# Attention and top-1 experts on one core: score columns packed, and the order of TensorE written over pairs of heads

## The chip, the core and the metric

One NeuronCore of one Trainium2 chip runs the whole program. The metric is the device time of one execution in microseconds. Three runs of the kernel before gave 333.72, 333.74 and 530.59 us; the median is 333.74 us.

## The reference

Four batches of eight heads attend over 768 tokens with 64 values a head; then every token passes a gate to one of eight experts. `is_retrieval` is `[1, 0, 1, 0, 0, 0, 1, 0]`: heads 0, 2 and 6 see all earlier keys ("full" heads here), the other five see the last 64 keys and the first four, the sinks ("streaming" heads).

```python
scores = scale * np.matmul(q, k.transpose(0, 1, 3, 2))
causal = rel >= 0
stream_keep = causal & (is_sink | in_win)     # is_sink: key < 4, in_win: rel < 64
...
a = np.exp(scores)
a = a / (np.sum(a, axis=-1, keepdims=True) + 1e-09)
out = np.matmul(a, v)
...
x = out.transpose(0, 2, 1, 3).reshape(B * S, H * D)
do_compute = (x @ w_skip) > 0
e_idx = np.argmax(x @ w_gate, axis=1)         # of the tokens in do_compute
h = np.maximum(xc[mask] @ w1[e], 0.0)
y[mask] = gate_w[mask, None] * (h @ w2[e])
out[do_compute] = xc + y
```

## The kernel before

The function `tile_duo_attention_split__then__moe_early_exit_skip_kernel` works in three stages.

**Attention** (lines 369 to 513) loops over four batches and, in each, over four pairs of heads, sixteen pairs in all. GpSimd issues the loads of q and k with a cast to fp16 (lines 378 and 381) and, for every second pair, two tiles of expert weights of 1 MB each, cast likewise (lines 415 and 416), all on its one DMA queue. SyncE (SP) issues the loads of v in fp32 (line 384) and the stores of a batch's output (line 516). TensorE (PE) transposes q and k, 24 small transposes a pair (line 392); ScalarE (ACT) copies qT (line 399), VectorE (DVE) kT (line 403), GpSimd casts v (line 409).

For each head, `qk_exp` takes one key block of 128 and a stretch of up to 512 queries: a matmul gives the scores in PSUM with the keys along the partitions (line 433, tile `pst`, two buffers), ScalarE takes the exponential into `ats` (line 439), VectorE multiplies the blocks on the diagonal and beside it with masks (lines 442 and 465). A streaming head has for each key block its own and the next query block, and a row group of its own for the four sink keys, 4 rows by 512 queries. Then line 484 weighs: for each query block the matmuls of `ats` with v and a column of ones add up in `opsa`, and VectorE divides (lines 491 and 492).

After each pair GpSimd casts the output (line 498), PE transposes it (line 503), and line 510 adds the pair's part to the gate's logits. After each batch VectorE chooses experts and gives every token a place in a list of 256 slots per expert (lines 518 to 589).

**Routing** (lines 591 to 623) turns the lists into gather and scatter indices (`idx_g` in line 611, `idx_s` in line 613).

**Experts** (lines 625 to 690): GpSimd gathers sixteen tiles of 128 tokens (line 636); `first(e)` casts and transposes tokens (line 652) and multiplies with `w1` (line 662); `second(e)` multiplies with `w2` (line 673), adds to the tokens on VectorE (line 677), and scatters the rows back (line 679). Each scatter waits for the one before. `general_path` is taken only if a list overflows or `is_retrieval` differs; with these inputs it is not.

The order of the work on each engine is set by a scheduler that follows the order of the code and what is ready; pools with a number of buffers limit how far it runs ahead.

## Time and profile before

| what | value |
|---|---|
| median of 3 runs | 333.74 us |
| profiled execution, its own time | 336.85 us |
| its span, first to last instruction | 335.3 us |
| PE busy | 260.9 us, 78% |
| DVE busy | 150.0 us, 45% |
| ACT busy | 123.9 us, 37% |
| POOL busy | 102.7 us, 31% |
| read from HBM, written | 56.64 MB, 10.49 MB |

The span is from the first to the last instruction on the core; the time of an execution also holds what lies around it. A busy share is a mean over stages that differ, so the stages are read one by one. The ends of matmuls are modelled; their starts are measured.

### The profile page before, as it was taken

What the parts mean: (1) busy time and instruction counts of PE and PEld (TensorE: products, weight loads), DVE (VectorE), ACT (ScalarE), POOL (GpSimd) and SP (SyncE); (2) the same over time, 40 slices, a digit from 0 to 9 for tenths busy, and PEclk for the clock granted to TensorE, in tenths of its full rate; (3) what the DMA queues carried; (4) which work ended last, traced back from release to release, by engine and by line L of the source; (5) the groups of instructions that cost most, each with busy time, mean ns of one, the idle gap of its engine ahead of it and who ended that gap; (6) DMA issues with size and microseconds to landing.
All of it is one profiled execution on the core that took longest, in us unless ns stands there. A gap on an engine that the chain in (4) does not pass through costs nothing.

```text
span 335.3 us, 5082 instructions
## 1 busy us (share of the span) xinstructions
PE 260.9 (78%) x1844; PEld 144.6 (43%) x1844; DVE 150.0 (45%) x619; ACT 123.9 (37%) x289; POOL 102.7 (31%) x161
## 2 busy tenths in 40 slices
PE   0297999966999995899998599995318899999600
PEld 0143645532445543354454244443215667776200
DVE  1223553438554554747435855644821244332300
ACT  1054454424654551645353455552002232333000
POOL 8920241443224326032131020200067523222320
PEclk9999999999999999999999999999999999999955
DMA  6999979799999999999743600002346601110010
GB/s 95 145 204 204 198 126 189 123 217 229 207 204 195 202 197 228 259 203 195 122 87 57 203 1 0 3 0 80 111 128 188 186 18 73 48 71 32 18 38 2
DMA packets 53122, 42.64 MB, mean 127 GB/s; under 512 B 27931, under 2 KB 44315, under 8 KB 53090
## 3 DMA queue, kind: packets, MB, share of 16 engines
q0 software_dynamic: 24864, 29.66, 48.1%
q1 hardware_dynamic: 28226, 12.59, 16.6%
q8 instruction: 16, 0.26, 0.3%
q14 instruction: 16, 0.13, 0.1%
HBM read 56.64 MB, written 10.49 MB: 200 GB/s over the span
## 4 chain that ended last, share of the span: by engine, by line
PE 60%; DMA 15%; DVE 7%; ACT 5%; POOL 5%; issue 5%; POOLq 0%; DVEq 0%; ACTq 0%
PE pst L433 18%; PE opsa L484 14%; DMA qin<-in_q_dram 8%; PE hps L662 7%; DMA out_dram<-xg,idx_s 6%; PE yps L673 5%; ACT ats L439 5%; PE kTps L392 5%; PE qTps L392 4%; PE gxtp L503 3%; PE gps L510 1%; DMA xg<-out_dram,idx_g 1%; PE xtp L652 1%; POOL va L409 1%; POOL gx L498 1%
## 5 line engine op out<-in xcount | busy, mean ns | idle before, releaser
L439 ACT ACTIVATE ats<-pst 128x256 f16<-128x256 f32 (+4 forms) x236 | 91.5, 418 | 95.3 <-PE pst L433 93.6
L433 PE MATMUL pst<-qT,kT 64*128 64x256 f16 (+4 forms) x236 | 88.8, 426 | 6.1 <-ACT ats L439 3.9
L484 PE MATMUL opsa<-va,ats 128*128 128x65 f16 x552 | 66.6, 240 | 3.7 <-ACT ats L439 2.5
L484 PEld LDWEIGHTS <-ats 128*128 128x128 f16 x552 | 38.7, 116 | 59.9 <-DVE ats L442 16.8
L409 POOL CAST va<-vf 128x768 f16<-128x768 f32 x16 | 13.7, 859 | 87.8 <-PE opsa L484 40.5
L665 ACT ACTIVATE ht<-hps 128x512 f16<-128x512 f32 x32 | 18.9, 598 | 55.7 <-PE hps L662 51.5
L392 PE MATMUL qTps<-ident,qin 128*64 128x128 f16 x192 | 22.7, 314 | 16.1 <-DMA qin<-in_q_dram 16.1
L662 PE MATMUL hps<-xT,w1a 128*128 128x256 f16 x256 | 31.7, 286 | 1.9 <-issue 1.9
L673 PE MATMUL yps<-w2a,ht 128*128 128x512 f16 x128 | 29.9, 379 | 0.5 <-DVE xg L677 0.5
L442 DVE TENSOR_TENSOR ats<-ats,retr_diag 128x128 f16<-128x128 f16 x72 | 16.1, 239 | 31.7 <-ACT ats L439 31.4
L433 PEld LDWEIGHTS <-kT 64*128 64x128 f16 (+1 forms) x236 | 19.3, 102 | 25.0 <-issue 15.2
L662 PEld LDWEIGHTS <-w1a 128*128 128x128 f16 x256 | 26.3, 103 | 7.6 <-issue 2.1
L679 POOL DMA_INDIRECT out_dram<-xg,idx_s x16 | 15.9, 995 | 43.3 <-DMA out_dram<-xg,idx_s 30.1
L392 PE MATMUL kTps<-ident,kin 128*64 128x128 f16 x192 | 26.8, 314 | 3.0 <-DMA kin<-in_k_dram 3.0
L442 DVE TENSOR_TENSOR ats<-ats,strm_dn 128x128 f16<-128x128 f16 x100 | 24.9, 249 | 7.6 <-ACT ats L439 6.9
L677 DVE SCALAR_TENSOR_TENSOR xg<-yps,gsl,xg 128x512 f32<-128x512 f32 x16 | 11.9, 750 | 36.3 <-PE yps L673 36.3
L498 POOL CAST gx<-xb 128x768 f16<-128x768 f32 x16 | 13.3, 831 | 47.8 <-DVE xb L492 47.8
L392 PEld LDWEIGHTS <-qin 128*64 128x64 f16 x192 | 15.6, 161 | 20.1 <-DMA qin<-in_q_dram 16.7
L392 PEld LDWEIGHTS <-kin 128*64 128x64 f16 x192 | 17.0, 159 | 11.0 <-issue 6.0
L636 POOL DMA_INDIRECT xg<-out_dram,idx_g x16 | 16.6, 1036 | 15.8 <-DVE idx_s L613 11.2
L403 DVE COPY kT<-kTps 128x768 f16<-128x768 f16 x16 | 15.3, 958 | 12.4 <-PE kTps L392 10.3
L491 DVE RECIPROCAL rec<-opsa 128x6 f32<-128x6 f32 x32 | 6.3, 196 | 28.0 <-PE opsa L484 27.3
(123 smaller groups left out, 227.2 us busy)
## 6 DMA issues: line engine op xcount, KB each, us to landing
w1a<-in_moe_w_dram POOLq DMA_DIRECT2D x8, 1024.0 KB
w2a<-in_moe_w_dram POOLq DMA_DIRECT2D x8, 1024.0 KB
vf<-in_v_dram SPq DMA_DIRECT2D x32, 192.0 KB, 9.0
out_dram<-xb SPq DMA_DIRECT2D x4, 1536.0 KB, 7.6
qin<-in_q_dram POOLq DMA_DIRECT2D x16, 192.0 KB
kin<-in_k_dram POOLq DMA_DIRECT2D x16, 192.0 KB
xg<-out_dram,idx_g POOLq DMA_INDIRECT x16
out_dram<-xg,idx_s POOLq DMA_INDIRECT x16
```

The costliest lines, as they stand in the source:

```text
L392: nc.tensor.matmul(dn[hd * D:(hd + 1) * D, n], src[:, hd, n * D:(n + 1) * D], C.ident, is_transpose=True, start=(n == 0), stop=(n == NQB - 1))
L409: nc.gpsimd.tensor_copy(va[:, :, :, :D], vf)
L433: nc.tensor.matmul(pst[:k_rows, :qn], kTh[:, j * P:j * P + k_rows], qTh[:, q_lo:q_hi], start=True, stop=True)
L439: nc.scalar.activation(dst, pst[:k_rows, :qn], ACT.Exp)
L442: nc.vector.tensor_mul(ats[:k_rows, sl, q_lo:q_lo + mw], ats[:k_rows, sl, q_lo:q_lo + mw], diag_mask[:k_rows, :mw])
L484: nc.tensor.matmul(opsa[:, i, :], ats[:kr, sl, i * QB:i * QB + QB], vh[:kr, j, :], start=(cnt == 1), stop=(cnt == total))
L498: nc.gpsimd.tensor_copy(x16, xb[:, :, h0:h0 + 2].rearrange("p n h d -> p n (h d)"))
L636: nc.gpsimd.indirect_dma_start(out=xg, out_offset=None, in_=out[:, :], in_offset=bass.IndirectOffsetOnAxis(ap=idx_g[:, t:t + 1], axis=0), ...
L662: nc.tensor.matmul(hps[:, fi, :], w1a[:, e, s, fs * P:(fs + 1) * P], xT[:, s, :], start=(s == 0), stop=(s == DS - 1))
L665: nc.scalar.activation(ht[:, 2 * f2:2 * f2 + 2], hps, ACT.Relu)
L673: nc.tensor.matmul(yps, hts[e][:, fs, s2 * P:(s2 + 1) * P], w2a[:, e, fs, :], start=(fs == 0), stop=(fs == FS - 1))
L679: nc.gpsimd.indirect_dma_start(out=out[:, :], out_offset=bass.IndirectOffsetOnAxis(ap=idx_s[:, t:t + 1], axis=0), in_=xgs[t], in_offset=No ...
```

## The change

Scores are packed. A full head's 21 blocks of 128 by 128 lie one after another in 2688 columns, the six diagonal blocks first; a streaming head's eleven blocks in 1408. They are computed in chunks of 1024 columns, each with one exponential, and the tile `pst` holds 1024 columns, two buffers as before. For a streaming head the four sink keys take over the first four rows of the blocks beside the diagonal (keys there that the window leaves out), and `vx` is v with its first four rows changed to match; so there is no row group for the sinks, and their weighting matmuls are gone. One mask instruction covers a chunk of a streaming head, or the six diagonal blocks of a full one.

q and k are loaded in fp32 by SP, two pairs of buffers, and cast by GpSimd with both heads side by side, so that one transpose of 128 by 128 serves both heads: 12 a pair. The transposes of q and k, of the gate and the counts of the routing share one PSUM buffer (`tps`).

The order on PE is written out over pairs: in iteration i stand the scores of pair i, the transposes of pair i + 1, the weighting of pair i - 1 and the gate of pair i - 2. The other engines are ordered by the scheduler. Output is stored by half batches. The weight tiles are tiles of their own; `load_weights` asks for them as the loop goes, and the last expert's two tiles lie in a pool that opens after attention. Two of five masks move into `general_path`, the rest are built after the first casts.

```diff
-    C.retr_diag = band_mask(nc, const, "retr_diag", 0, 0, None)
-    C.strm_d0 = band_mask(nc, const, "strm_d0", 0, 0, WINDOW - 1, sink=True)
-    C.strm_dn = band_mask(nc, const, "strm_dn", 0, 0, WINDOW - 1)
-    C.strm_s0 = band_mask(nc, const, "strm_s0", QB, 0, WINDOW - 1, sink=True)
-    C.strm_sn = band_mask(nc, const, "strm_sn", QB, 0, WINDOW - 1)
-
 
     lneg = const.tile([P, P], FP16, name="lneg")
...
-    w1a = wpool.tile([P, E, DS, F], FP16, name="w1a")
-    w2a = wpool.tile([P, E, FS, DM], FP16, name="w2a")
+    wts = {}
+
+    def wtile(e, half, pool):
+        t = pool.tile([P, DS * F], FP16, name=f"w{half + 1}_{e}")
+        wts[e, half] = (t.rearrange("p (s f) -> p s f", s=DS) if half == 0
+                        else t.rearrange("p (s d) -> p s d", s=FS))
+
+    for e in range(E - 1):
+        for half in range(2):
+            wtile(e, half, wpool)
...
+    todo = [(e, half) for e in range(E) for half in range(2)]
+
+    def load_weights(upto):
+        while todo and len(todo) > 2 * E - upto:
+            e, half = todo.pop(0)
+            nc.gpsimd.dma_start(out=wts[e, half], in_=(w1r, w2r)[half][e])
...
+    RCOL, pos = {}, NQB * P
+    for j in range(NQB):
+        RCOL[j, j] = j * P
+        for i in range(j + 1, NQB):
+            RCOL[j, i] = pos
+            pos += P
+    RLEN = pos
+    SLEN = (2 * NQB - 1) * P
+    CH = 1024
...
+        vab.append(const.tile([P, 2, NQB, D + 1], FP16, name=f"va{i}"))
+        nc.gpsimd.memset(vab[i][:, :, :, D:D + 1], 1.0)
+        vxb.append(const.tile([P, 2, NQB - 1, D + 1], FP16, name=f"vx{i}"))
+
+    with tc.tile_pool(name="ld", bufs=2) as ld_pool, \
+         tc.tile_pool(name="qk_in", bufs=1) as qk_in_pool, \
          tc.tile_pool(name="qt", bufs=2) as qt_pool, \
-         tc.tile_pool(name="va", bufs=2) as v_pool, \
-         tc.tile_pool(name="xsb", bufs=1) as x_pool, \
+         tc.tile_pool(name="xsb", bufs=3) as x_pool, \
...
+        def load_qk(i):
+            b, hs = heads(i)
+            for name, src in (("q", qv), ("k", kv)):
+                f = ld_pool.tile([P, 2, NQB, D], FP32, tag=name + "f",
+                                 name=name + "f")
+                nc.sync.dma_start(out=f.rearrange("p h n d -> p h (n d)"),
+                                  in_=src[b, :, hs[0]:hs[0] + 2])
+                qk32[name, i] = f
+
+        def load_v(i):
+            b, hs = heads(i)
+            vf = ld_pool.tile([P, 2, NQB, D], FP32, tag="vf", name="vf")
+            for hi, hh in enumerate(hs):
+                nc.sync.dma_start(out=vf[:, hi], in_=vv[b, :, hh])
+            v32[i] = vf
+
+        def cast_qk(i):
+            for name in ("q", "k"):
+                h16 = qk_in_pool.tile([P, NQB, 2, D], FP16, tag=name + "in",
+                                      name=name + "in")
+                nc.gpsimd.tensor_copy(
+                    h16, qk32[name, i].rearrange("p h n d -> p n h d"))
+                qk16[name, i] = h16
+
+        def cast_v(i):
+            va, vx = vab[i % 2], vxb[i % 2]
+            nc.gpsimd.tensor_copy(va[:, :, :, :D], v32[i])
+            for hi, hh in enumerate(heads(i)[1]):
+                if not IS_RETR[hh]:
+                    nc.gpsimd.tensor_copy(vx[:, hi], va[:, hi, :NQB - 1])
+                    nc.gpsimd.tensor_copy(
+                        vx[:N_SINK, hi], va[:N_SINK, hi, 0:1].to_broadcast(
+                            [N_SINK, NQB - 1, D + 1]))
+
+        def transpose(i, name):
+            tps = tr_psum.tile([P, S], FP16, tag="tps", name="tps")
...
+        def pieces(retr):
+
+
+            work = [(i * P, i, i, 1) for i in range(NQB)]
+            if retr:
+                for j in range(NQB - 1):
+                    work.append((RCOL[j, j + 1], j, j + 1, NQB - 1 - j))
+            else:
+                for i in range(1, NQB):
+                    work.append(((NQB - 1 + i) * P, i - 1, i, 1))
+                work.append((NQB * P, -1, 1, NQB - 1))
+            cut = []
+            for (c, j, i, n) in work:
+                while n:
+                    m = min(n, 4 - (c // P) % 4)
+                    cut.append((c, j, i, m))
+                    c, i, n = c + m * P, i + m, n - m
+            return cut
...
+        def score(i, hi, c0):
+            retr = IS_RETR[heads(i)[1][hi]]
+            r = slice(hi * D, (hi + 1) * D)
+            cn = min(CH, (RLEN if retr else SLEN) - c0)
+            pst = st_psum.tile([P, CH], FP32, tag="pst", name="pst")
+            for (c, j, qb, n) in pieces(retr):
+                if c0 <= c < c0 + CH:
+                    kr = P if j >= 0 else N_SINK
+                    kc = max(j, 0) * P
+                    nc.tensor.matmul(
+                        pst[:kr, c - c0:c - c0 + n * P],
+                        qkT["k", i][r, kc:kc + kr],
+                        qkT["q", i][r, qb * P:(qb + n) * P],
+                        start=True, stop=True)
+            b0 = base(i, hi) + c0
+            ac = ats[i][:, b0:b0 + cn]
+            nc.scalar.activation(ac, pst[:, :cn], ACT.Exp)
+            if not retr:
+                nc.vector.tensor_mul(
+                    ac, ac,
+                    smask.rearrange("p n c -> p (n c)")[:, c0:c0 + cn])
+            elif c0 == 0:
+                dg = ats[i][:, b0:b0 + S].rearrange("p (n c) -> p n c", n=NQB)
+                nc.vector.tensor_mul(
+                    dg, dg, C.retr_diag.unsqueeze(1).to_broadcast(
+                        [P, NQB, P]))
+
+        def weigh(i, hi):
+            b, hs = heads(i)
+            b0 = base(i, hi)
+            va, vx = vab[i % 2], vxb[i % 2]
+            if IS_RETR[hs[hi]]:
+                plan = [(qb, RCOL[j, qb], va[:, hi, j])
+                        for qb in range(NQB) for j in range(qb + 1)]
+            else:
+                plan = []
+                for qb in range(NQB):
+                    plan.append((qb, qb * P, va[:, hi, qb]))
+                    if qb:
+                        plan.append((qb, (NQB - 1 + qb) * P,
+                                     vx[:, hi, qb - 1]))
...
+            for n, (qb, c, vb) in enumerate(plan):
+                nc.tensor.matmul(
+                    opsa[:, qb, :], ats[i][:, b0 + c:b0 + c + P], vb,
+                    start=(n == 0), stop=(n == len(plan) - 1))
+            if i % 2 == 0 and hi == 0:
...
             ohf = oh.rearrange("p e n -> p (e n)")
             W = E * NQB
-            kps = st_psum.tile([P, 512], FP32, tag="pst", name="kps")
+            kps = tr_psum.tile([P, 256], FP32, tag="tps", name="kps")
...
+        with tc.manual_schedule(engines={mybir.EngineType.PE}):
+            load_qk(0)
+            load_v(0)
+            load_qk(1)
+            load_v(1)
+            cast_qk(0)
+            smask = make_masks()
+            load_qk(2)
+            transpose(0, "q")
+            transpose(0, "k")
+            cast_qk(1)
+            for i in range(NPR + 2):
+                cur = chunks(i) if i < NPR else []
+                if i < NPR:
+                    cast_v(i)
+                if i + 3 < NPR:
+                    load_qk(i + 3)
+                if i + 2 < NPR:
+                    load_v(i + 2)
+                load_weights(min(i // 2, 2 * E - 2))
+
+                def step(n):
+                    if n < len(cur):
+                        score(i, *cur[n])
+
+                step(0)
+                if i + 1 < NPR:
+                    transpose(i + 1, "q")
+                step(1)
+                if i >= 2:
+                    gate_transpose(i - 2)
+                if 1 <= i <= NPR:
+                    weigh(i - 1, 0)
+                step(2)
+                if i + 1 < NPR:
+                    transpose(i + 1, "k")
+                if i + 2 < NPR:
+                    cast_qk(i + 2)
+                step(3)
+                if 1 <= i <= NPR:
+                    weigh(i - 1, 1)
+                step(4)
+                if i >= 2:
+                    if (i - 2) % 4 == 0 and i > 2:
+                        place((i - 2) // 4 - 1)
+                    gate_logits(i - 2)
+            place(B - 1)
+
...
+    with tc.tile_pool(name="moe_w", bufs=1) as mw_pool, \
+         tc.tile_pool(name="moe_x", bufs=2) as mx_pool, \
...
+
+        for half in range(2):
+            wtile(E - 1, half, mw_pool)
+        load_weights(2 * E)
 
```

The functions `choose` and `place` hold the lines of the routing per batch as they were; `gate_transpose` and `gate_logits` those of the gate.

PE, before, in the middle of attention (`ats` exponentials, `opsa` weighted sums, `qTps` and `kTps` transposes): scores, weighting and transposes follow each other in ones and twos.

```order
L433 LDWEIGHTS kT
L433 MATMUL pst<-qT,kT 128x256
L484 LDWEIGHTS ats
L484 MATMUL opsa<-va,ats 128x65
L392 LDWEIGHTS qin
L392 MATMUL qTps<-ident,qin 64x128
L433 LDWEIGHTS kT
L433 MATMUL pst<-qT,kT 128x256
L392 LDWEIGHTS qin
L392 MATMUL qTps<-ident,qin 64x128
```

PE after, in an iteration: the last chunk of scores of a streaming head, with the sinks as a piece of 4 rows, then the weighting of the pair before, in one row.

```order
L517 LDWEIGHTS kT
L517 MATMUL pst<-qT,kT 128x128
L517 LDWEIGHTS kT
L517 MATMUL pst<-qT,kT 4x384
L552 LDWEIGHTS at
L552 MATMUL opsa<-va_129,at 128x65
L552 LDWEIGHTS at
L552 MATMUL opsa<-va_129,at 128x65
L552 LDWEIGHTS at
L552 MATMUL opsa<-vx_131,at 128x65
L552 LDWEIGHTS at
L552 MATMUL opsa<-va_129,at 128x65
```

What moved: before, the weighting of a head stands behind that head's own exponentials; after, it stands between the chunks of the next pair.

GpSimd (POOL) before, in attention: the loads of q and k are issued here, between the weight tiles `w1a` and `w2a`.

```order
L415 DMA w1a<-in_moe_w_dram 128x4x1024
L416 DMA w2a<-in_moe_w_dram 128x8x512
L378 DMA qin<-in_q_dram 128x2x384
L381 DMA kin<-in_k_dram 128x2x384
L415 DMA w1a<-in_moe_w_dram 128x4x1024
L409 CAST va<-vf 128x12x64
L498 CAST gx_1051<-xb 128x768
L410 MEMSET va 128x12
L378 DMA qin<-in_q_dram 128x2x384
L381 DMA kin<-in_k_dram 128x2x384
L416 DMA w2a<-in_moe_w_dram 128x8x512
```

POOL after, one iteration: casts of q, k, v, the copies into `vx`, the cast of the output `gx`, and one weight tile.

```order
L568 CAST gx_1242<-xh 128x768
L452 CAST va_126<-vf 128x12x64
L446 CAST qin<-qf 128x768
L455 COPY vx_128<-va_126 128x325
L359 DMA w_4_120<-in_moe_w_dram 128x4x1024
L456 COPY vx_128<-va_126 4x325
L446 CAST kin<-kf 128x768
L568 CAST gx_1373<-xh 128x768
L452 CAST va_129<-vf 128x12x64
L446 CAST qin<-qf 128x768
L455 COPY vx_131<-va_129 128x325
L359 DMA w_4_121<-in_moe_w_dram 128x8x512
```

What moved: the loads of q and k are no longer in this queue, their casts are; one weight tile is issued in each iteration, for the fourteen of the first seven experts.

POOL before, at the start of the experts: the gathers `xg` follow the last cast directly.

```order
L498 CAST gx_2829<-xb 128x768
L498 CAST gx_2996<-xb 128x768
L636 DMA xg_3160<-out_dram,idx_g 128x512
L636 DMA xg_3164<-out_dram,idx_g 128x512
L636 DMA xg_3168<-out_dram,idx_g 128x512
L636 DMA xg_3172<-out_dram,idx_g 128x512
```

POOL after, at the same place.

```order
L568 CAST gx_2356<-xh 128x768
L568 CAST gx_2421<-xh 128x768
L777 DMA xg_2605<-out_dram,idx_g 128x512
L359 DMA w_7_2595<-in_moe_w_dram 128x4x1024
L359 DMA w_7_2596<-in_moe_w_dram 128x8x512
L777 DMA xg_2609<-out_dram,idx_g 128x512
L777 DMA xg_2613<-out_dram,idx_g 128x512
L777 DMA xg_2617<-out_dram,idx_g 128x512
```

What moved: the two tiles of the last expert stand between the first gather and the second.

## Rows read from the trace of the kernel before

**Rows 1.** Windows: PE, PEld, DVE, ACT, POOL busy (count); TensorE clock, DMA share, GB/s.

```profile
17.00:160.00 143.00, 128.06 (x898) 65.95 (x898) 75.80 (x327) 67.95 (x167) 44.59 (x67) 1.00 1.13 199
90.00:130.00 40.00, 38.36 (x282) 20.67 (x281) 20.08 (x75) 18.56 (x46) 14.72 (x23) 1.00 1.21 201
160.00:231.00 71.00, 63.72 (x437) 31.57 (x436) 38.55 (x171) 34.74 (x87) 9.76 (x16) 1.00 0.24 54
244.00:335.30 91.30, 63.18 (x448) 42.80 (x448) 23.31 (x48) 18.91 (x32) 32.50 (x32) 0.90 0.24 74
```

**Rows 2.** Line 503, the gate transposes, and the chain's two pieces of them.

```profile
L503 PE MATMUL gxtp<-ident,gx x96: 286/314/314, 38.8 to 233.6; 128*128 128x128 f16 x96
...
128.69 0.83 PE gxtp L503 x6
...
233.08 0.83 PE gxtp L503 x6
```

**Rows 3.** The page's chain that ended last, shares of the span by line.

```profile
PE pst L433 18%; PE opsa L484 14%; DMA qin<-in_q_dram 8%; PE hps L662 7%; DMA out_dram<-xg,idx_s 6%; PE yps L673 5%; ACT ats L439 5%; PE kTps L392 5%; PE qTps L392 4%; PE gxtp L503 3%; PE gps L510 1%; DMA xg<-out_dram,idx_g 1%; PE xtp L652 1%; POOL va L409 1%; POOL gx L498 1%
```

**Rows 4.** Groups by line and shape: count, busy us, mean ns, idle before, releasers.

```profile
L439 ACT ACTIVATE ats<-pst 128x256 f16<-128x256 f32 x124 | 44.3, 382 | 52.2 <-PE pst L433 51.8
...
L673 PE MATMUL yps<-w2a,ht 128*128 128x512 f16 x128 | 29.9, 379 | 0.5 <-DVE xg L677 0.5
...
L442 DVE TENSOR_TENSOR ats<-ats,strm_dn 128x128 f16<-128x128 f16 x100 | 24.9, 249 | 7.6 <-ACT ats L439 6.9
...
L433 PE MATMUL pst<-qT,kT 64*128 64x512 f16 x36 | 21.8, 605 | 1.2 <-ACT ats L439 1.0
...
L439 ACT ACTIVATE ats<-pst 128x512 f16<-128x512 f32 x36 | 21.5, 597 | 22.8 <-PE pst L433 22.1
...
L465 DVE TENSOR_TENSOR ats<-ats,strm_sn 128x128 f16<-128x128 f16 x80 | 17.9, 223 | 0.0
...
L409 POOL CAST va<-vf 128x768 f16<-128x768 f32 x16 | 13.7, 859 | 87.8 <-PE opsa L484 40.5 <-issue 36.0 <-PE pst L433 11.4
```

**Rows 5.** The page's 40 slices, the line of the TensorE clock.

```profile
PEclk9999999999999999999999999999999999999955
```

**Rows 6.** Timeline, PE: weighting of two heads, gate transposes, transposes of an expert.

```profile
193.20 1.06 PE L484 MATMUL opsa<-va,ats 128*128 128x65 f16 x16
...
196.60 1.39 PE L484 MATMUL opsa<-va,ats 4*128 4x65 f16 x10
...
202.31 0.82 PE L503 MATMUL gxtp<-ident,gx 128*128 128x128 f16 x6
...
274.93 0.61 PE L652 MATMUL xtp<-ident,x 128*128 128x128 f16 x8
```

**Rows 7.** The page's DMA queues: packets, MB, share of sixteen engines' span.

```profile
q0 software_dynamic: 24864, 29.66, 48.1%
q1 hardware_dynamic: 28226, 12.59, 16.6%
```

**Rows 8.** Timeline of the start: first mask, first issue of q, first scores.

```profile
3.72 0.23 POOL L49 MEMSET retr_diag<- 128x128 f16 x1
...
8.77 0.72 POOL L378 DMA_DIRECT2D qin<-in_q_dram  x1
...
17.94 0.82 PE L433 MATMUL pst<-qT,kT 64*128 64x512 f16 x2
```

**Rows 9.** Timeline from the last pair to the second expert's matmuls.

```profile
231.25 0.20 DVE L491 RECIPROCAL rec<-opsa 128x6 f32<-128x6 f32 x1 [2.22 <-PE opsa L484]
...
242.99 0.17 DVE L611 TENSOR_TENSOR idx_g<-tok,egs 128x16 int32<-128x16 f32 x1
...
251.46 6.08 PE L662 MATMUL hps<-xT,w1a 128*128 128x256 f16 x32
...
260.26 1.91 PE L662 MATMUL hps<-xT,w1a 128*128 128x256 f16 x16 [1.85 <-issue]
```

**Rows 10.** Line 384, the loads of v: from issue to landing.

```profile
DMA to landing us min/median/max: 2.5/9.0/23.8
```

239 lines of the change are left out of this document (101 added, 138 removed).

## The prediction

> **What bounds the kernel now.** I read the view of the windows first, then the queues, then the chain that ended last, and last the timeline at three places.
>
> The windows cut the span into three stages [rows 1]. From 17 to 160 us the DMA engines are full (share 1.13, and 1.21 in the stretch 90:130; over 1 because packets of two queues overlap). From 160 to 231 us the same attention work runs on with a share of only 0.24. From 244 us on the experts run. So the weights are all in by about 160 us. Does the stage go faster once the DMA engines are free? No: the gate transposes, six for each of the sixteen pairs of heads, run from 38.8 to 233.6 us, and the groups at 128.69 and 233.08 us are the eighth and the sixteenth [rows 2]. The last eight steps take 104.4 us, 13.05 each; the first seven, in the full stretch, (128.69 - 38.8)/7 = 12.8. Attention is therefore bound by its own chain of small steps, not by transfers: the chain's line shares have PE scores at 18%, PE weighting at 14%, the exponential behind them at 5%, and 8% in waits for q [rows 3]. The exponential of 256 columns takes 382 ns and ScalarE stood idle 52 us before 124 of them, for the scores [rows 4]: the two score buffers hand over too often.
>
> The clock line of the page shows 9 from the start [rows 5], yet rows of one shape disagree with it: 512 columns take 605 ns in the scores and 379 ns in the experts [rows 4], and six gate transposes take 0.82 us where eight in the experts take 0.61 [rows 6]. The difference of 226 ns is about 512 columns at 1.2 against 2.4 GHz. I take the whole attention stage as running at the lower level: one transpose takes 314 ns [rows 2], so (0.82 - 0.31)/5 = 0.102 us for each 128 columns.
>
> **The change part by part.**
>
> Score and weighting work on PE, per pair with one full and one streaming head (three of four pairs). Scores: 21 blocks of 128 columns for the full head, 11 plus 5 blocks of sink columns for the streaming one, 37 x 0.102 = 3.8 us. Transposes: 12 of q and k (before 24 of half the width) and 6 for the gate, 18 x 0.102 = 1.8. Weighting: 21 + 11 = 32 matmuls; sixteen take 1.06 us when all 128 rows are used, 0.066 each, 2.1 us; ten of the present mix with 4-row sinks take 1.39, twice that per matmul [rows 6], and the 80 sink matmuls of the kernel go. Gate logits 0.2, an estimate. Sum 7.9 us; a pair of two streaming heads 32 x 0.102 + 1.8 + 22 x 0.066 + 0.2 = 6.7; mean 7.6. PE now stands in written order, and the transposes of q, of the gate and of k share one buffer; I add six hand-overs of 0.15 us and half a microsecond for the copy of qT, an estimate: 9.0 us per iteration. Against 13.05 that is the gain by itself.
>
> The other engines per iteration: exponentials of 1024, 640 and 384 columns at (597 - 382)/256 = 0.84 ns a column [rows 4] are 1.03, 0.70 and 0.49 us, 4.3 us for a pair. Masks on VectorE: 292 instructions of 128 columns at 223 to 249 ns become 52 long ones. No row has the long form; at most 17 blocks x 0.249 = 4.2 us a pair (as dear per block as now), at least one instruction's fixed part, near zero per block; either way VectorE stays near 7 to 9 us with its copies and routing. GpSimd gets two casts more (q and k, 0.86 us each by the cast of v [rows 4]) and one or two pairs of small copies (0.15 to 0.86 each), and loses two q/k DMA issues of 0.72: 5 to 6 us. All this stays under the next term, which hides it; without that cover PE's 9.0 us decides.
>
> Transfers. The loads of q and k move from GpSimd's queue, where they stood behind 1 MB weight tiles, to SP's queue, behind v. The waits for q (8% of the chain) go. What is late next: the work itself. The two queues took 48.1% and 16.6% of sixteen engines' span, 161 and 56 us [rows 7]. Gathers and scatters are most of the last window (91 us x 0.24 = 22 us), so 139 us carry 16.8 MB of weights and 6.3 MB of q and k (as written), 6.0 us a MB: 6.3 us for a tile, 2.4 for the q and k of a pair. SP's 12.6 MB of v and output cost 56 us, 3.5 us for a pair's share. The change issues one tile per pair, for fourteen pairs. So an iteration carries 12.2 us of engine time; at the share of 1.13 that the long full window reached, 10.8 us. That is more than PE's 9.0. The unknown in it is q and k as fp32 without cast: the same bytes read, twice the bytes written. Below: the cast's 2.4 us; above: 0.79 MB at SP's 4.4 us a MB, 3.5 us. I take 2.4, since v's many 256-byte pieces make the upper row dear; the upper end adds 1.0 us to an iteration, 13 us in all.
>
> The start. GpSimd builds five masks, 20 instructions, from 3.72 us on, and issues q at 8.77 [rows 8]; now SP issues q at once, and the casts of q and k come ahead of the masks: 8.77 less 4.4 us of masks and two casts of 0.86 make 6.1, and after transposes and copies the first scores stand near 9.5 us instead of 17.94. GpSimd alone paces iteration 0: 14 instructions for masks at 0.22 (3.1), their copies (2 x 0.86 + 0.5), four casts (3.4), small copies 0.7: iteration 1 starts near 15.5 us.
>
> The end. From the last reciprocal (231.25) to the gather indices (242.99) the routing takes 11.7 us [rows 9]; that chain is the same. In the experts one thing changes: the tiles of expert 7 are issued on GpSimd's queue behind the first gather and ahead of the other fifteen. Two tiles are 12.6 us of engine time, say 11; the second gather lands some 9 us later, an estimate. Now the first expert's matmuls begin at 251.46, run slowly for 6 us, and the next start at 260.26 after a wait of 1.85 [rows 9]; of the 9 us, about 3 fall into that slack: 6 us are lost. Bounds: 0 (if the gathers overtake) to 12.
>
> Sum: 15.5 + 13 iterations x 10.8 (140.4) + two without weights x 9.0 (18) + the last weighting 5 + routing 11.7 = 190.6 us to the indices, now 243.0. From there to the end 92.3 us (335.3 less 242.99) [rows 9], plus 6: a span of 289. The profiled execution has 1.55 us outside its span, 290.5; it was 3.1 us above the median shown, so 287 us.
>
> **The rivals.**
>
> A: transfers don't pace. If the loads ahead (two pairs deep) and a better packing of plain loads hide them, PE's 9.0 us decides: 15.5 + 135 + 5 + 11.7 + 98.3 = 265.5, or 264 us as median. For it: the DMA engines are idle at first and 160:231 shows that attention needs little; against it: those 13 iterations bring 13 of the 16 tiles and most loads, which filled the window to 160 us before [rows 1]. If the TensorE clock also rises, the stage is still held by transfers, and only the last iterations gain, 8 us. The Trainium skill, "TensorE: Matmul & The Clock Gate" (why this matters for your kernels), says that sustained matmul activity gives the higher clock; the trace agrees only in the experts, where the rows fall from 605 to 379 ns, and the denser order here could bring it into attention.
>
> B: the shared engines serve the queues in turn, so that v's small pieces each wait behind a large packet of weights. Loads of v landed in 2.5 us at best, 9.0 in the middle and 23.8 at worst [rows 10]. With two loads of v and q and k in every iteration late by 1.5 us more than their share, an iteration is 12.3 us: 15.5 + 160 + 18 + 16.7 + 98.3 = 308.5, 307 us. The Trainium skill, "DMA: Bandwidth & Descriptors" (queues, rings and completion order), says the engines go round the queues packet by packet; that would make this the expected course, and the trace fits with 23.8 against 2.5 us. Against it: a tile has 512 or 1024 packets and a pair's loads 2048, so half of the loads run without weights beside them.
>
> C, slower: the written order locks PE and GpSimd together. The cast of the next q and k needs the transposes done (one buffer), the transposes need the cast, and a gate transpose needs GpSimd's cast of x. If these lie end to end, 9.0 + 6.0 = 15 us: 15.5 + 15 x 15 + 16.7 + 98.3 = 355.5, 354 us. It decides from 13.7 us an iteration on. Against it: the casts are issued most of an iteration ahead, and nothing else is queued on GpSimd for more than 6 us.
>
> That the change does not do what it says I can see only in the weights: if the tiles come later than one a pair, expert 7's wait grows to 12 us, inside the range.
>
> **How the numbers follow.** Forecast 0.58 (own range 272 to 302: the bounds of q/k, of the gather and of PE's hand-overs), A 0.18, B 0.17, C 0.07. Holding 8 in 10, the range runs from 258, just under A, to 314, above B. A measurement of this kernel can tell about 2% from no change, 327 to 340 us. Forecast, A and most of B are faster: 0.88; B's far end and the mild part of C fall within 2%: 0.06; the rest of C slower: 0.06.
>
> **What would show it.** Right: DMA share near 1.1 from 17 to about 155 us and then low; pairs 10 to 11.5 us apart while tiles flow and about 9 after; gather indices near 190 us; the second gather about 10 us after the first; ScalarE's 1024 columns at 1.03 us. Wrong: a DMA share well below 1 with pairs over 11 us apart (then C, or an engine is the bound); pairs under 9 us while tiles flow (A); 512 columns at 379 ns in the attention stage; a gather that does not wait.

## The result and the profile after

The changed kernel takes 280.26 us (median of 4 runs, 277.9 to 282.8) against 333.87 us in the same comparison: a ratio of 0.837, 95% interval 0.829 to 0.845. Forecast were 287 us, range 258 to 314. The profiled execution took 282.8 us, 281.1 of them its span. Ratios, here and below, compare only runs within 1.5% of their kernel's fastest, while medians are of all runs; the profiled execution of the kernel after is the slowest of its four.

From the page of the kernel after: the span, the TensorE clock and the DMA share in 40 slices, and the two large queues.

```profile
span 281.1 us, 4592 instructions
...
PEclk9999999995555575555556555555559999999995
DMA  7999999999999999999999950309985011111010
...
q0 software_dynamic: 16160, 23.37, 43.2%
q1 hardware_dynamic: 40066, 25.17, 32.5%
```

The DMA line answers to [rows 1] and the queues to [rows 7]: 43.2% and 32.5% of 281.1 us are 121 and 91 us, 213 in all, where before it was 161 and 56, 217. The change moved transfers from one queue to the other and took none away. They now fill the line from the start to about 165 us, as before to 160; only what comes behind them is shorter. The clock line now falls to 5 at about 63 us, but the six gate transposes take 0.80 us at 29.8 us, where it shows 9, and 0.82 at 134 us, where it shows 5 (0.82 in [rows 6]); all sixteen groups take 0.80 to 0.82. So apart from short spells the stage ran at 1.2 GHz all along, as the prediction read it.

From the same page, the chain that ended last, by engine and by line:

```profile
PE 35%; DMA 34%; DVE 13%; POOL 6%; issue 3%; ACT 3%; SPq 2%; POOLq 0%; DVEq 0%; ACTq 0%
DMA vf<-in_v_dram 12%; DMA qf<-in_q_dram 12%; PE hps L803 11%; PE yps L814 9%; PE pst L517 6%; DMA xg<-out_dram,idx_g 5%; DMA kf<-in_k_dram 4%; PE opsa L552 3%; PE tps L463 2%; DVE at L531 2%; POOL gx L568 2%; PE xtp L580 2%; DMA out_dram<-xg,idx_s 2%; DVE oh L90 2%; ACT at L524 1%
```

Where [rows 3] had scores and weighting on PE, with 18% and 14%, the loads of v, q and k now have 28% together.

Windows of the kernel after (columns as in [rows 1]).

```profile
17.00:56.00 39.00, 37.15 (x327) 25.31 (x326) 23.80 (x41) 20.78 (x27) 22.31 (x30) 1.00 1.15 239
29.80:56.10 26.30, 26.03 (x236) 18.09 (x236) 15.74 (x29) 13.51 (x18) 15.14 (x21) 1.00 1.16 248
56.00:156.00 100.00, 74.84 (x734) 52.70 (x734) 68.09 (x168) 43.39 (x57) 48.55 (x69) 0.58 1.08 239
160.00:187.00 27.00, 14.21 (x166) 10.71 (x163) 19.05 (x96) 4.95 (x8) 4.31 (x6) 0.50 0.30 79
190.00:281.10 91.10, 62.73 (x448) 42.75 (x448) 23.50 (x48) 19.10 (x32) 31.42 (x32) 0.84 0.35 94
```

Its line of gate transposes, as in [rows 2] (count, ns at least, median and most, first and last start).

```profile
L580 PE MATMUL xtp<-ident,gx x96: 263/314/314, 29.8 to 176.6; 128*128 128x128 f16 x96
```

The sixteen groups of gate transposes start at 29.8, 38.2, 46.9, 56.1, then on average every 11.1 us to 155.8, and the last three at 164.8, 171.6 and 176.1. PE is busy 99% of the second window, which holds three steps, and 75% of the third. The last gate transpose, at 233.6 us before, starts at 176.6. The routing behind it is what it was: the last division at 174.3, the gather indices at 186.0, 11.7 us as in [rows 9].

Groups by form of the kernel after (busy us, mean ns of one, idle before and its releaser), to be held against [rows 4].

```profile
L524 ACT ACTIVATE at<-pst 128x1024 f16<-128x1024 f32 x44 | 44.9, 1023 | 48.7 <-PE pst L517 48.5
...
L526 DVE TENSOR_TENSOR at<-at,smask 128x1024 f16<-128x1024 f16 x20 | 16.0, 798 | 1.6 <-ACT at L524 1.5
L452 POOL CAST va<-vf 128x768 f16<-128x768 f32 x16 | 14.4, 903 | 43.8 <-DMA vf<-in_v_dram 26.5 <-PE pst L517 14.3 <-PE opsa L552 3.0
...
L531 DVE TENSOR_TENSOR at<-at,retr_diag 128x768 f16<-128x768 f16 x12 | 14.0, 1165 | 13.3 <-ACT at L524 13.3
```

The exponential is as forecast (1.03 us). Among the casts it is that of v that waits, three times and 26.5 us, for its load. The last mask row is odd: 768 columns take longer than 1024; that comes back at the end.

The start of the experts in the timeline of the kernel after (start, busy, engine, line; in brackets the idle time before it and its releaser).

```profile
187.25 1.10 POOL L777 DMA_INDIRECT xg<-out_dram,idx_g  x1 [11.22 <-DVE idx_s L749]
188.36 1.71 POOL L359 DMA_DIRECT2D w<-in_moe_w_dram  x2
190.37 1.08 POOL L777 DMA_INDIRECT xg<-out_dram,idx_g  x1 [0.30 <-issue]
190.74 0.43 DVE L790 CAST x<-xg 128x512 f16<-128x512 f32 x1 [4.45 <-DMA xg<-out_dram,idx_g]
...
204.23 1.01 POOL L777 DMA_INDIRECT xg<-out_dram,idx_g  x1 [4.87 <-DMA w<-in_moe_w_dram]
204.68 0.43 DVE L790 CAST x<-xg 128x512 f16<-128x512 f32 x1 [12.38 <-DMA xg<-out_dram,idx_g]
...
206.32 6.10 PE L803 MATMUL hps<-xT,w 128*128 128x256 f16 x32
```

The second gathered tile is there 13.9 us after the first, behind two weight tiles in the same queue, and the first products begin 20 us after the indices; before it was 8.5 [rows 9].

### The profile page after: what moved, and what is told of

It is laid out like the page before. It is cut to its first block, busy times and chain, and to the rows that moved or that the text cites. A ratio compares the mean times of both kernels' runs of the same rounds, so it can differ in the third digit from the quotient of the medians.

```text
span 281.1 us, 4592 instructions
## 1 busy us (share of the span) xinstructions
PE 200.7 (71%) x1764; PEld 139.6 (50%) x1764; DVE 145.2 (52%) x378; ACT 95.4 (34%) x129; POOL 126.6 (45%) x184
## 3 DMA queue, kind: packets, MB, share of 16 engines
q0 software_dynamic: 16160, 23.37, 43.2%
q1 hardware_dynamic: 40066, 25.17, 32.5%
## 4 chain that ended last, share of the span: by engine, by line
PE 35%; DMA 34%; DVE 13%; POOL 6%; issue 3%; ACT 3%; SPq 2%; POOLq 0%; DVEq 0%; ACTq 0%
DMA vf<-in_v_dram 12%; DMA qf<-in_q_dram 12%; PE hps L803 11%; PE yps L814 9%; PE pst L517 6%; DMA xg<-out_dram,idx_g 5%; DMA kf<-in_k_dram 4%; PE opsa L552 3%; PE tps L463 2%; DVE at L531 2%; POOL gx L568 2%; PE xtp L580 2%; DMA out_dram<-xg,idx_s 2%; DVE oh L90 2%; ACT at L524 1%
## 5 line engine op out<-in xcount | busy, mean ns | idle before, releaser
L524 ACT ACTIVATE at<-pst 128x1024 f16<-128x1024 f32 (+2 forms) x76 | 62.7, 832 | 76.0 <-PE pst L517 75.8
L517 PE MATMUL pst<-qT,kT 64*128 64x128 f16 (+4 forms) x428 | 72.5, 323 | 3.5 <-DVE kT L474 3.5
L517 PEld LDWEIGHTS <-kT 64*128 64x128 f16 (+1 forms) x428 | 36.9, 122 | 22.8 <-issue 14.2
L452 POOL CAST va<-vf 128x768 f16<-128x768 f32 x16 | 14.4, 903 | 43.8 <-DMA vf<-in_v_dram 26.5
L803 PE MATMUL hps<-xT,w 128*128 128x256 f16 x256 | 31.7, 286 | 0.0
L552 PE MATMUL opsa<-va,at 128*128 128x65 f16 x372 | 30.0, 242 | 0.0
L814 PE MATMUL yps<-w,ht 128*128 128x512 f16 x128 | 29.9, 379 | 0.0
L552 PEld LDWEIGHTS <-at 128*128 128x128 f16 x472 | 27.7, 131 | 3.9 <-issue 3.3
L803 PEld LDWEIGHTS <-w 128*128 128x128 f16 x256 | 26.3, 103 | 5.6
L526 DVE TENSOR_TENSOR at<-at,smask 128x1024 f16<-128x1024 f16 (+1 forms) x40 | 26.5, 686 | 1.6 <-ACT at L524 1.5
L568 POOL CAST gx<-xh 128x768 f16<-128x768 f32 x16 | 14.7, 921 | 23.3 <-DVE xh L560 23.3
## 6 DMA issues: line engine op xcount, KB each, us to landing
vf<-in_v_dram SPq DMA_DIRECT2D x32, 192.0 KB, 13.1
```

The source lines that it names most:

```text
L517: nc.tensor.matmul(pst[:kr, c - c0:c - c0 + n * P], qkT["k", i][r, kc:kc + kr], qkT["q", i][r, qb * P:(qb + n) * P], start=True, stop=True)
L524: nc.scalar.activation(ac, pst[:, :cn], ACT.Exp)
L526: nc.vector.tensor_mul(ac, ac, smask.rearrange("p n c -> p (n c)")[:, c0:c0 + cn])
L552: nc.tensor.matmul(opsa[:, qb, :], ats[i][:, b0 + c:b0 + c + P], vb, start=(n == 0), stop=(n == len(plan) - 1))
L568: nc.gpsimd.tensor_copy(x16, xh[:, :, h2:h2 + 2].rearrange("p n h d -> p n (h d)"))
L803: nc.tensor.matmul(hps[:, fi, :], wts[e, 0][:, s, fs * P:(fs + 1) * P], xT[:, s, :], start=(s == 0), stop=(s == DS - 1))
```

## The experiments

Theory T: while tiles flow, attention is paced by its transfers. Its main rival E: by engines and their hand-overs. Theory L: expert 7's tiles in front of the gathers cost 6 us. V, Q and P came up on the way. Ratios are to the kernel before, run on the same chip; the kernel after has 0.837 (0.829 to 0.845).

### Twelve tiles left out

```diff
-todo = [(e, half) for e in range(E) for half in range(2)]
+todo = [(e, half) for e in (0, E - 1) for half in range(2)]
+# wts[1..6, half] = wts[0, half]
```

> Left out: the weight tiles of experts 1 to 6, twelve of sixteen; these experts compute with the tiles of expert 0. Theory T (transfers pace the middle of attention, 11.1 us a pair while tiles flow): without the tiles pairs come about 9 us apart throughout, nine steps of the middle are 2 us shorter each, and the whole takes 258 to 263 us against 280.3. Rival E (engines and their hand-overs pace): pairs stay near 11 us and the time stays within 276 to 284 us. Rival A2 (PE at the lower clock could go far below 9.0 us a pair): pairs under 8 us, under 250 us.

Measured: 261.8 us, ratio 0.780 (0.777 to 0.784). Its window over the middle of attention:

```profile
56.00:150.00 94.00, 80.32 (x857) 57.51 (x857) 72.05 (x212) 48.31 (x63) 46.62 (x63) 0.64 0.52 146
```

The gate transposes stand at 56.0 and, ten pairs on, at 145.2 us: 8.9 us a pair. PE is busy 85% of that, 7.6 us a pair. Not all of it ran at the lower clock: the granted clock has a mean of 0.64, where 0.50 is the lower level, and three of the groups of gate transposes (at 63.2, 99.8 and 137.2 us) take 0.49 to 0.50 us instead of 0.80 to 0.82. But the three steps from 28.6 to 56.0 us, with groups of 0.80 and 0.82 us, take 9.1 us each too. T holds, E falls, and A2 too. With half the DMA share a load of v lands in 4.7 us (median), where it takes 13.1 in the kernel after.

### Expert 7's tiles behind the gathers, and six tiles behind them

```diff
-        for half in range(2):
-            wtile(E - 1, half, mw_pool)
-        load_weights(2 * E)
         xgs = []
         for t in range(NT):
...
+        for half in range(2):
+            wtile(E - 1, half, mw_pool)
+        load_weights(2 * E)
```

> Changed: the two tiles of expert 7 are issued behind all sixteen gathers, not behind the first. Theory L (they hold up the second gather): the cast of the second gathered tile no longer waits 12.4 us, the first products begin about 8.5 us behind the indices as before the change, not 20, and the time falls by 6 us to 274 (bounds 269 to 278, since the first products then run at the lower clock). Rival: the wait only moves to expert 7's own products, and the time stays at 279 to 281 us.

Measured: 282.5 us, ratio 0.846 (0.839 to 0.852): no gain. The first products do begin at 191.9 us instead of 206.3, and those of expert 7 at 248.8 instead of 258.2. But the end is not set by products. From its timeline, the tiles and the first scatters:

```profile
205.86 1.82 POOL L359 DMA_DIRECT2D w<-in_moe_w_dram  x2
209.55 1.06 POOL L821 DMA_INDIRECT out_dram<-xg,idx_s  x1 [1.87 <-DVE xg L819]
222.48 1.02 POOL L821 DMA_INDIRECT out_dram<-xg,idx_s  x1 [11.87 <-DMA out_dram<-xg,idx_s]
225.39 0.98 POOL L821 DMA_INDIRECT out_dram<-xg,idx_s  x1 [1.88 <-DMA out_dram<-xg,idx_s]
```

Each scatter waits for the one before; the first was issued behind the two tiles, and the second waits 11.87 us for it. From 222.48 to the sixteenth at 269.39 they follow every 3.35 us. The wait had only moved, from the gathers to the scatters, which neither theory had named. With six tiles there (those of experts 5 to 7, moved in the same way):

> Changed: six weight tiles (experts 5 to 7) are issued behind the gathers; attention carries ten. Theory T with L: some 6 x 6 us of transfers leave attention, which then goes at PE's pace of about 9 us a pair in its second half; with the gathers no longer held up, 257 us (252 to 264). Rival E: only what the free gathers give, 274 us. Rival X: experts 5 to 7 then wait for their tiles, which come at some 6 us a tile behind the gathers, 268 us or more.

Measured: 293.0 us, ratio 0.875 (0.866 to 0.884). T's 257 and E's 274 us are missed; X has the number, 268 us or more, but not the reason, since the products of the last experts follow each other every 7.4 us as in the other kernels and wait for no tile.

```profile
195.31 5.08 POOL L359 DMA_DIRECT2D w<-in_moe_w_dram  x6
200.69 1.06 POOL L822 DMA_INDIRECT out_dram<-xg,idx_s  x1 [0.30 <-DVE x L792]
231.40 1.03 POOL L822 DMA_INDIRECT out_dram<-xg,idx_s  x1 [29.64 <-DMA out_dram<-xg,idx_s]
```

Attention ended 11 us earlier, as T wants it (first gather at 174.1 against 184.6 us with two tiles there), and the products of expert 7 began at 236.5 us. All of it, and more, is lost in one wait of 29.64 us between two scatters.

### Expert 7's tiles ahead of the gathers

The tiles take the buffers in which the exponentials of the last two pairs stood (8 KB a partition, the size of a tile), so that they are issued at 167.2 and 173.2 us.

```diff
+    at_pool = ctx.enter_context(tc.tile_pool(name="at", bufs=2))
...
+                if i >= NPR:
+                    wtile(E - 1, i - NPR, at_pool)
+                    load_weights(2 * E - 1 + i - NPR)
```

> Changed: the two tiles of expert 7 take the places of the exponentials of the last two pairs and are issued there, ahead of the gathers, where the DMA engines are half idle. Theory Q (whatever tiles stand in GpSimd's queue beside gathers or scatters hold up the one or the other; the sixteen scatters follow each other every 3.4 us): first scatter at about 209 us and none held up, 209.5 + 15 x 3.4 + 8 = 268.5 us of span, 270 us against 280.3. Rival: the transfers of the last pairs are held up instead, or another wait of 10 us shows in the experts, and the time stays at 278 to 282 us.

Measured: 275.1 us, ratio 0.819 (0.815 to 0.823): by the ratios 1.9% of 334 less than the kernel after, 6.2 us, by the medians 5.2, about the size that the prediction had for this place (L). Q's 270 us are not reached: the first products start at 193.2 us, but the first two experts take 10.2 and 9.7 us, the later ones 7.4: in that stretch PE waits 3.9 us, to 203.4 us, for the transposed tokens of a gathered tile, and the granted clock, back at the higher level at 196.9 us, is lower once more from 203.7 to 207.1 us.

### The casts of q and k on ScalarE, with the tiles as they fall and one by one

```diff
-                nc.gpsimd.tensor_copy(
-                    h16, qk32[name, i].rearrange("p h n d -> p n h d"))
+                nc.scalar.activation(
+                    h16, qk32[name, i].rearrange("p h n d -> p n h d"),
+                    ACT.Copy)
```

> Changed: the casts of q and k run on ScalarE, not on GpSimd. Theory P (VectorE instructions with two SBUF inputs are held while GpSimd works without a pause; the profile has four of 2.0 to 5.1 us in place of 0.2 to 0.6): the long ones go, since GpSimd has 27 us less to do, and the start of attention is some 4 us earlier; in the middle transfers pace and hide the rest: 275 us. Rival 1: the long ones are on the path everywhere: 268 us. Rival 2: ScalarE, with 32 casts of some 0.8 us between its exponentials, holds up TensorE: 282 us or more.

Measured: 297.1 us, ratio 0.882 (0.879 to 0.886). The number fits rival 2, its reason does not. From the waits (engine and line, for whom: us in all, times, longest):

```profile
POOL va L453 <- DMA vf<-in_v_dram: 63.1, 8, 13.8
...
ACT qin L446 <- DMA qf<-in_q_dram: 37.4, 7, 9.8
```

With GpSimd emptier, the scheduler issued the fourteen tiles by 111.5 us, two in an iteration, instead of by 152.9 us; the pairs then wait for their own loads, steps of 21.6, 16.6 and 17.2 us among them. (In both kernels the loop asks for a tile in every second iteration only, `i // 2`; the scheduler issued them earlier.) So the same edit was run again with GpSimd's order written and one tile in each iteration:

```diff
-        with tc.manual_schedule(engines={mybir.EngineType.PE}):
+        with tc.manual_schedule(engines={mybir.EngineType.PE,
+                                         mybir.EngineType.Pool}):
...
-                load_weights(min(i // 2, 2 * E - 2))
+                load_weights(min(i + 1, 2 * E - 2))
```

> Changed: the casts of q and k run on ScalarE, and GpSimd's order is written too, so that one weight tile is issued in each iteration (when only the casts moved, the tiles came two in an iteration in the first half, and the pairs waited for v and q up to 13.8 us). Theory T with its order of transfers (pairs starve when tiles run ahead): 274 to 281 us, as the kernel after or somewhat better, and no VectorE instruction of several us. Rival: ScalarE's casts hold up TensorE, 290 us or more even with the tiles one by one.

Measured: 276.4 us, ratio 0.823 (0.819 to 0.827), 21 us less by GpSimd's written order and, with it, the places of the tiles. Its control has this order and these tiles, but the casts on GpSimd:

> The control for the kernel with casts on ScalarE and one tile in each iteration (276.4 us): the same written order on GpSimd and the same tiles, but the casts of q and k stay on GpSimd. Theory P (GpSimd at work without a pause holds VectorE's instructions): instructions of 2 to 5 us are back on VectorE, and the time is that of the kernel after or a little over the control's partner, 279 to 284 us. Rival: the tiles' places alone made the difference, and the time is 275 to 278 us with the long instructions or without.

Measured: 279.7 us, ratio 0.834 (0.828 to 0.841). The casts' place is worth some 3 us, about 1%; the two intervals, each against the kernel before on its own chip, nearly touch. The group of the 1024-column mask in the control:

```profile
L526 DVE TENSOR_TENSOR at<-at,smask 128x1024 f16<-128x1024 f16 x20 | 20.9, 1046 | 3.2 <-ACT at L524 3.2
```

And with the casts on ScalarE:

```profile
L527 DVE TENSOR_TENSOR at<-at,smask 128x1024 f16<-128x1024 f16 x20 | 14.3, 715 | 6.9 <-ACT at L525 6.9
```

The mean is 331 ns less where GpSimd does not cast q and k, but not because each one is faster: the median is 0.68 us in both. Two of the twenty in the control take 2.95 us, and these make most of the difference of 6.6 us. In the kernel after, where GpSimd casts too, none of this group was held as long, and the mean is 798 ns.

### PE's order left to the scheduler

```diff
-        with tc.manual_schedule(engines={mybir.EngineType.PE}):
+        if True:
```

> Undone: the written order on PE; the scheduler orders it. Theory T (the middle is paced by transfers): the order on PE counts only in the start and the last pairs, 278 to 288 us. Rival O (the written order is what took pairs from 13 to 9 us): pairs 11 to 13 us apart also after the tiles are in, 295 us or more.

Measured: 266.5 us, ratio 0.790 (0.786 to 0.794): 14 us faster than with the written order. O falls (pairs 9.9 us apart on average between 56.9 and 155.9 us), and T, which had 278 to 288, is not complete. The difference lies in when the last pair's v is issued and how many tiles are issued ahead of it. In the kernel after, SP's two loads of the last v, and the fourteenth tile on POOL:

```profile
151.81 1.95 SPq L439 DMA_DIRECT2D vf<-in_v_dram  x2
...
152.90 0.89 POOL L359 DMA_DIRECT2D w<-in_moe_w_dram  x1
```

Without the written order: the last v, the twelfth tile, and the two behind it.

```profile
136.07 2.39 SPq L439 DMA_DIRECT2D vf<-in_v_dram  x2
...
137.16 0.89 POOL L359 DMA_DIRECT2D w<-in_moe_w_dram  x1
...
141.53 0.76 POOL L359 DMA_DIRECT2D w<-in_moe_w_dram  x1
...
152.13 0.89 POOL L359 DMA_DIRECT2D w<-in_moe_w_dram  x1
```

The fourteenth tile is issued at the same time in both. The last load of attention is issued 16 us earlier here, with two tiles behind it; in the kernel after, the fourteenth tile stands between its two halves and none behind. That gave theory V: what paces attention is not the sum of the transfers but those ahead of its own last load.

### The written order with the tiles later

Against the kernel with casts on ScalarE and one tile in an iteration, only the table of tiles changes:

```diff
-                load_weights(min(i + 1, 2 * E - 2))
+                load_weights((1, 2, 3, 4, 5, 6, 6, 7, 8, 9, 9, 10, 11, 12, 13, 14)[
+                    min(i, NPR - 1)])
```

> Against the kernel with casts on ScalarE and one tile in each iteration (276.4 us), only the iterations in which the tiles are issued change: twelve instead of fourteen by the time the last pair's v is issued, two more behind it. Theory V (the same transfers fill the DMA engines to the same end, but what attention waits for is its own loads, so that each tile issued behind them gives its 6.3 us of engine time back): 2 x 6.3 / 1.1 = 11 us less, 265 us (262 to 269). Rival: the sum of transfers alone counts, and the order among them not, 274 to 278 us.

Measured: 265.7 us, ratio 0.795 (0.791 to 0.798): 11 us, as V says. The last v with one tile in each iteration, and with the tiles later:

```profile
144.56 2.21 SPq L439 DMA_DIRECT2D vf<-in_v_dram  x2
...
134.52 3.73 SPq L439 DMA_DIRECT2D vf<-in_v_dram  x2
```

It is issued 10 us earlier, with twelve tiles ahead of it, as without a written order. With as many tiles ahead, the two orders of PE (with the casts on different engines) come out within 1 us of each other by the medians, 1.7 us by the ratios. In the middle of attention the granted clock rose as well, from 0.52 to 0.64; but without a written order all sixteen groups of gate transposes take 0.80 to 0.83 us, the lower clock, and the time is the same. So the higher clock is not needed for it; what it gave in this run was not separated.

### Both gains together

Expert 7's tiles ahead of the gathers (the edit above), once with the scheduler's order on PE, once with the written order and the later tiles:

> The scheduler's order on PE (266.5 us alone) together with expert 7's tiles issued ahead of the gathers (5 to 6 us alone). Theory Q and V: the two add up, 260 to 262 us. Rival: with attention 13 us shorter the transfers of the tiles end only with the first gathers, and the gain is lost again, 265 to 267 us.

> The written order with casts on ScalarE and the later tiles, and expert 7's tiles issued ahead of the gathers. Theory Q and V: 265 less 6, 259 us (256 to 264). Rival: four tiles then stand between the last loads and the first gather, 4 x 6.3 / 1.1 = 23 us, about as long as the rest of attention takes, so that the gathers wait, 264 to 270 us.

Measured: 261.8 us, ratio 0.786 (0.782 to 0.791), and 259.8 us, ratio 0.780 (0.776 to 0.784). In the first the interval overlaps that of the scheduler's order alone (0.786 to 0.794), so that a gain on top of it is not shown; in the second it is (0.795 before). This last kernel is 7% faster than the kernel after, and as fast with all sixteen tiles as the kernel after was without twelve of them. Its windows in the middle, at the end of attention and in the routing:

```profile
56.00:146.00 90.00, 76.44 (x798) 55.13 (x797) 67.59 (x181) 56.37 (x76) 38.45 (x53) 0.79 1.14 260
146.00:160.00 14.00, 9.57 (x120) 7.59 (x118) 9.10 (x40) 4.09 (x5) 6.16 (x9) 0.50 1.03 188
160.00:173.00 13.00, 2.27 (x20) 1.36 (x18) 7.77 (x51) 0.24 (x1) 1.16 (x2) 0.50 0.99 190
```

The DMA share stays at 1 through the routing, where the kernel after had 0.30 between 160 and 187 us, and the first gather is issued at 172.4 us, 2.6 us behind the indices (1.2 in the kernel after). The rival's long wait of the gathers did not come. The profiled execution, 256.3 us, is the fastest of the four.

### Exponentials of 512 columns

```diff
-            nc.scalar.activation(ac, pst[:, :cn], ACT.Exp)
+            for x0 in range(0, cn, 512):
+                x1 = min(x0 + 512, cn)
+                nc.scalar.activation(ac[:, x0:x1], pst[:, x0:x1], ACT.Exp)
```

> Undone in part: each chunk's exponential is cut into pieces of 512 columns. 44 exponentials of 1024 columns and 20 of 640 become two each, ScalarE has 64 fixed parts of 0.17 us more, 11 us in all. Theory T: hidden while transfers pace, 280 to 283 us. Rival: ScalarE stands in the chain of every pair (scores, exponential, weighting), 287 us or more.

Measured: 281.98 us in one run and 286.4 to 287.1 in three, a median of 286.5 and no interval. It stays open whether the width of the exponential counts here.

## Why the prediction was right, step by step

**What bounded the kernel before.** That attention was bound by its chain at the lower clock, not by transfers, is borne out: at the same lower clock the three steps in the window 29.80:56.10 take 8.8 us each, and that with a DMA share of 1.16, where the last eight steps before took 13.05 [rows 2], though the share was 0.24 from 160 us on [rows 1]. The windows also show where the gain lies. Before, PE was busy 63.72 of 71.00 us from 160 to 231 us [rows 1], 11.7 us of each step; now it is 26.03 of 26.30, 8.7 us of each step. So of the 4.3 us some 3 are work that PE no longer has, and the rest are waits, as far as ends that are modelled tell this. Which part of the packing took the work away was not separated, and that the two score buffers handed over too often was not tested. The written order it was not, as far as the whole time shows, since the scheduler's order goes as fast.

**PE's 9.0 us.** As a total it is right at the lower clock: 8.8 us a step in that window, and 9.1 in the same steps of the kernel without twelve tiles. Its parts are not. The sum had 7.6 us of work and 1.4 of hand-overs; the window shows 8.7 busy and 0.1 not, and without a written order, where all gate transposes ran at the lower clock, PE is busy 9.1 of 9.9 us a pair:

```profile
56.90:155.90 99.00, 90.55 (x827) 62.44 (x827) 72.29 (x202) 46.63 (x62) 50.70 (x73) 1.00 1.13 246
```

That the window 56:150 without twelve tiles gives 7.6 busy and 1.3 not, nearly the sum's figures, is luck: part of it ran at the higher clock, where the sum has the lower one.

**The other engines.** The exponential at 1.03 took 1.023 us; masks cost (16.0 + 11.5 + 14.0) / 16 = 2.6 us a pair (the middle form, 384 columns, has 11.5 us), inside the bound of 4.2; GpSimd 48.55 us in nine pairs, 5.4, between 5 and 6. VectorE 7.6, between 7 and 9.

**The transfers.** The packet records of the trace, grouped by size, give 6.3 us of engine time for a tile, 2.4 for q and k of a pair and 3.3 for v and output, against 6.3, 2.4 and 3.5. Of the two bounds for q and k the lower was right. A pair in the middle took 11.1 us at a share of 1.08, 12.0 us of engine time against 12.2. The pace was forecast at 10.8. One step of this part failed: the waits for q, 8% of the chain before, were to go. In the kernel after the chain has 12% in q, 12% in v and 4% in k. The transfers that pace the stage show here as waits for these loads, though q and k no longer stand behind the weight tiles in their queue.

**The step that was too coarse** is that every tile paces the iteration in which it is issued, as if all transfers ahead of the end counted alike. It came out in this kernel because about one tile stands in each iteration down to the last load. Two tiles behind the last load gave 11 us back. All fourteen issued by 111.5 us cost 17 us against the kernel after and 21 against one tile in each iteration. The prediction had the sum right and did not ask for whom the last of the transfers are needed.

**The start.** First scores at 10.35 us, forecast 9.5; the second iteration's at 18.46, forecast 15.5. The first mask was held 4.5 us (below), but that is not the reason: with the casts on ScalarE and one tile in each iteration this mask takes 1.13 us, and the second iteration still starts at 17.80 us. So GpSimd alone did not pace iteration 0, as the prediction has it: the iteration took 8.1 to 8.5 us, as long as the next ones.

**How the errors add up.** The start was 3.0 us late. The way from there to the last division took 155.8 us instead of 163.4: the first three steps of 8.5 to 9.2 us, although tiles flowed and the DMA share was 1.16, the next nine of 11.1 on average, and the last three of 8.9, 6.8 and 4.5. Transfers paced nine steps and not thirteen, each dearer than the 10.8 forecast, and that 13 x 10.8 came near is in part luck. The indices came at 186.0 us instead of 190.6.

**The gathers.** The size was right, the working was not. The second tile came after 13.9 us, not 9. The first products began 11.8 us later behind the indices than before, and of that 1.9 us were won back up to the second expert's (6.9 us from one to the other instead of 8.8), not the 3 of the prediction. Some more were won back at the end, where the last scatter starts 8.1 us behind the last product before and 5.6 now. The last scatters, before and after:

```profile
323.60 0.98 POOL L679 DMA_INDIRECT out_dram<-xg,idx_s  x1 [2.64 <-DMA out_dram<-xg,idx_s]
...
272.98 0.98 POOL L820 DMA_INDIRECT out_dram<-xg,idx_s  x1 [2.54 <-DMA out_dram<-xg,idx_s]
```

From the indices to the last scatter it was 80.6 us before and is 87.0 now, 6.3 more (6 forecast); in the run with the tiles ahead of the gathers it is 80.1. But from the last scatter to the end of the span it was 11.7 us and is 8.1, and no row shows why, so that from the indices to the end it is 95.1 us, only 2.8 more than before [rows 9]. The prediction had 98.3.

**The rivals.** A's 264 us is what the kernel takes where the tiles don't pace (261.8), and by the prediction's own sign, pairs under 9 us while tiles flow, A holds for two of the first three steps. There the clock had not risen; later it rose in spells, longer ones without the twelve tiles. B's late loads were there, v landing in 13.1 us with tiles and 4.7 without, and it is such loads that the chain waits for, but a pair took 11.1 us, not 12.3. Nothing like C's 15 us showed. Its one true part is that engines hold each other back through shared buffers: the cast of v waited for PE 17.3 us in all.

## What to carry to other kernels

Where transfers fill a stage, ask of each one which step needs it and when, and put those that the stage doesn't need behind its own last load, by a written order; a scheduler that sees no dependency puts them where an engine is free. Where weight tiles were issued just ahead of gathers or scatters on their queue, they held them up: two tiles a gather for 13.9 us or a chain of scatters for 11.9, six the scatters for 29.6. Issue such a load in a stretch where the queue has nothing else that is needed soon, and look for buffers that come free in time. And change one place at a time: moving a cast moved fourteen loads, and the time told of those.

## What was not expected of the hardware

VectorE's instructions with two inputs in SBUF can be held for several us while GpSimd works. In the kernel after, the first mask on VectorE, and GpSimd's instructions beside it:

```profile
12.47 5.07 DVE L531 TENSOR_TENSOR at<-at,retr_diag 128x768 f16<-128x768 f16 x1 [2.18 <-ACT at L524]
...
12.40 0.82 POOL L446 CAST kin<-kf 128x768 f16<-128x768 f32 x1
13.17 1.59 POOL L452 CAST va<-vf 128x768 f16<-128x768 f32 x2
14.71 0.45 POOL L455 COPY vx<-va 128x325 f16<-128x325 f16 x1
15.12 0.82 POOL L446 CAST qin<-qf 128x768 f16<-128x768 f32 x1
15.89 0.45 POOL L456 COPY vx<-va 4x325 f16<-4x325 f16 x1
16.29 0.45 POOL L455 COPY vx<-va 128x325 f16<-128x325 f16 x1
16.69 0.77 POOL L359 DMA_DIRECT2D w<-in_moe_w_dram  x1
```

At its shortest this mask takes 0.56 us. Here it takes 5.07 and ends as GpSimd turns from casts and copies to issuing a load. Three others of the kind, of 3.9, 3.2 and 2.0 us, are instructions of 6 and 48 columns in the choice of experts, lines 89 and 90. With the casts on ScalarE and the tiles one by one, the longest mask takes 1.13 us and none of the others is held as long, and the control, with the casts on GpSimd, has two of 2.95. So the long ones come with the casts of q and k on GpSimd. The place of these casts is worth some 3 us in this kernel; how much of that the held instructions cost was not separated. The Trainium skill, "SBUF — State Buffer" (who interferes with whom), says that a VectorE instruction with two SBUF inputs contends with a GpSimd instruction that reads SBUF, and that the loser is blocked for the other's whole instruction. The trace agrees and goes further: the wait lasted over seven instructions in a row.

The sixteen scatters, each behind the one before, have a pace of their own: behind the long waits they follow every 3.35 us with two tiles and every 3.46 with six, some 50 us for fifteen. The products of an expert, two tiles of tokens, come every 7.4 us, 3.7 a tile, so that scatters once held up hardly catch up. And the higher TensorE clock came late after a stage at the lower one: with expert 7's tiles ahead of the gathers, products ran from 193.2 us on; the granted clock rose at 196.9, fell at 203.7 after PE's wait of 3.9 us, and stayed at the higher level only from 207.1 us.
